# One head of each pair in whole float32 in the first attention stage, and fewer transfers for the score operands

## The chip, the cores and the metric

The kernel runs on one core of one Trainium2 chip. The metric is the device time of one execution in microseconds (us), as the median of several runs. The engines of the core work side by side and meet through semaphores: PE multiplies matrices into PSUM, DVE and ACT read PSUM and SBUF, POOL works on SBUF alone, and SP here issues nearly all transfers, in the fixed order of its queue.

## The reference

Attention for 4 batches of 12 heads, 448 positions and head size 64, followed by two mixers over the joined heads. Only the attention part and the outline of the mixers matter here:

```python
def rmsnorm(x, g):
    rms = np.sqrt(np.mean(x * x, axis=-1, keepdims=True) + 1e-06)
    return x / rms * g
q_n, k_n = (rmsnorm(q, g_q), rmsnorm(k, g_k))
scores = (1.0 / np.sqrt(q.shape[-1])) * np.matmul(q_n, k_n.transpose(0, 1, 3, 2))
attn = np.exp(scores - np.max(scores, axis=-1, keepdims=True))
attn = attn / (np.sum(attn, axis=-1, keepdims=True) + 1e-09)
x = np.matmul(attn, v)          # then (4, 448, 768)
# first mixer:  u = x + (U, V mixing over positions); x = u + relu(u @ w_ch1) @ w_ch2   (768 -> 3072 -> 768)
# second mixer: u = x + relu mixing over positions;   x = u + relu(u @ w_ch1) @ w_ch2   (768 -> 1536 -> 768)
```

The channel weights of the mixers arrive as float64 and are turned into float32 on the chip by a chain on ACT, DVE and POOL (`to_f32`, lines 113 to 135).

## The kernel before, in words

A product that must be good to float32 is made of float32r products. An operand x is split into `hi`, the value rounded to float32r, and `lo`, the rest; a product of two split operands is `hi*hi + lo*hi + hi*lo`, three matmuls that add up in one PSUM bank (lines 523 to 525 for the mixers). A float32r product of 448 columns is one row `128x448` of PE in the profile.

The attention works on pairs of heads: `load_pair` (line 241) loads q, k and v of two heads, normalises q and k (squares and scaling on POOL, sums on DVE), and splits v into `vs` (line 281, ACT and POOL). `turn_pair` (line 284) transposes q and k on PE, splits them out of PSUM (ACT writes `hi`, DVE writes `lo`), and then stacks them by SBUF-to-SBUF transfers on SP: for each head `qs` is [q_hi; q_lo], `ks` is [k_hi; k_hi] and `kt` is [k_lo; k_lo], each 128 partitions of which the upper and the lower 64 are one transfer (lines 310 to 313). That is 12 transfers of 112 KB a pair, and two matmuls of depth 128 then make the scores: `qs*ks + qs*kt` (lines 324 and 325).

`softmax` (line 318) makes, for each of 4 chunks of 112 rows, the scores, the negated maximum on DVE (line 327), the exponential with its sum on ACT (line 329), and scales by the reciprocal on POOL (line 336). `weigh` (line 339) transposes the probabilities on PE into `pt`, 4 blocks of 112x112 a chunk, copies them out as `ph` (ACT, line 363) and `pl = pt - ph` (DVE, line 367), and multiplies twice: `vs` holds v_hi and v_lo side by side in its 128 columns, so `ph*[v_hi, v_lo]` and `pl*[v_hi, v_lo]` give all four parts, and line 375 (ACT) and line 376 (DVE) add the lower half of the result to the upper one.

`weigh` already has a branch for heads named in `whole`: p and v stay in float32 and one matmul a chunk takes the place of two. In the kernel before no pair names any head (lines 750 and 751).

The program has four stages. In the first, the **lone stage**, the 24 heads of batches 0 and 1 run with nothing else beside them but the loads of some weights (until about 213 us). At the seam the first weights of the mixer are loaded and converted and its first products start. In the second stage the mixer of batches 0 and 1 runs on PE, with the 24 heads of batches 2 and 3 spread between its products; then come the second mixer and both mixers of batches 2 and 3.

The order on each engine isn't that of the source: a scheduler of the build simulates the program with its own costs and writes out a fixed order for each engine, SP included. An instruction that must wait holds up all that stand behind it on its engine. Buffers set when that happens: q and k have 2 each, v 3, `vs` 2, the stacked operands 3 each, and the turned `hi` and `lo` one each. The load of v of a later pair (line 247) waits in SP's queue until a buffer of v is free.

Of the kernel before, what the change touches and what calls it, by code (L numbers as in the profile page):

```python
# [10 lines left out]
F32R = mybir.dt.float32r  # L11
U32 = mybir.dt.uint32
I64 = mybir.dt.int64
AF = mybir.ActivationFunctionType
# [10 lines left out]
def attention_then_two_mixers(  # L25
# [30 lines left out]
    nc = tc.nc  # L56
    P = 128
    B, H, S, D = q.shape
    DM = out.shape[2]
    CP, NC4 = 112, 4  # L60
# [14 lines left out]
    def f(x):  # L75
        return x.bitcast(F32)

    def mm(o, l, r, start, stop):
        nc.tensor.matmul(o, lhsT=l, rhs=r, start=start, stop=stop)  # L79
# [20 lines left out]
    pools = {"late": False, "split_u": nc.gpsimd}  # L100
# [140 lines left out]
    def load_pair(b, hp, whole, mul):  # L241
        h0 = 2 * hp
        raw = []
        for nm, src in (("q", q), ("k", k), ("v", v)):
            t = pools["at"].tile([CP, 2, NC4, D], F32, tag=f"{nm}r", bufs=AT[nm + "r"],
                        name=f"{nm}r")
            nc.sync.dma_start(t, src[b, h0:h0 + 2].rearrange("h (p c) d -> p h c d", c=NC4))
            raw.append(t)
        qr, kr, vr = raw

        ms = pools["at"].tile([CP, 2, 8], F32, tag="ms", name="ms")
        for i, t in enumerate((qr, kr)):
            sq = pools["at"].tile([CP, 2 * NC4, D], F32, tag="sq", bufs=AT["sq"], name="sq")
            tt = t.rearrange("p h c d -> p (h c) d")
            mul(sq, tt, tt)
            nc.vector.reduce_sum(ms[:, i], sq, axis=AX.X)
        nc.gpsimd.tensor_scalar(ms, ms, 1.0 / D, 1e-6, op0=ALU.mult, op1=ALU.add)
        rs = pools["at"].tile([CP, 2, 8], F32, tag="rs", name="rs")
        nc.scalar.activation(rs, ms, AF.Ln)
        nc.scalar.activation(rs, rs, AF.Exp, scale=-0.5)  # L260
        nt = pools["at"].tile([CP, 2, 8], F32, tag="nt", name="nt")
        nc.gpsimd.tensor_mul(nt, rs, rs)
        nc.gpsimd.tensor_mul(nt, nt, ms)
        nc.gpsimd.tensor_scalar(nt, nt, -0.5, 1.5, op0=ALU.mult, op1=ALU.add)
        nc.gpsimd.tensor_mul(rs, rs, nt)

        def scale(i, shape):
            return rs[:, i].rearrange("p (h c) -> p h c", h=2).unsqueeze(3).to_broadcast(shape)

        qn, kn = [], []  # L270
        for i, (nm, t, n) in enumerate((("qn", qr, qn), ("kn", kr, kn))):
            n.append(pools["at"].tile([CP, NC4, 2, D], F32, tag=nm, bufs=AT["qn"], name=nm))
            mul(
                n[0].rearrange("p c h d -> p h c d"), t, scale(i, [CP, 2, NC4, D]))
        qn, kn = qn[0], kn[0]

        vs = pools["at"].tile([CP, 2, NC4, 2, D], F32R, tag="vs", bufs=AT["vs"], name="vs")
        js = [j for j in range(2) if j not in whole]
        if js:
            js = slice(js[0], js[-1] + 1)  # L280
            split(vr[:, js], vs[:, js, :, 0], vs[:, js, :, 1])
        return qn, kn, [vr[:, j] if j in whole else vs[:, j] for j in range(2)]

    def turn_pair(qn, kn):

        parts = []
        for n, scale in ((qn, gg), (kn, None)):
            tt = psum("t", [P, S], "tt")
            for c in range(NC4):
                nc.tensor.transpose(  # L290
                    tt[:, c * CP:(c + 1) * CP], n[:, c].rearrange("p h d -> p (h d)"),
                    ident[:CP, :CP])
            hi = pools["at"].tile([P, S], F32R, tag="qh" if scale else "kh",
                                  bufs=1, name="hi")
            lo = pools["at"].tile([P, S], F32R, tag="ql" if scale else "kl",
                                  bufs=1, name="lo")
            if scale:
                nc.scalar.activation(hi, tt, AF.Copy, scale=scale)
                nc.vector.scalar_tensor_tensor(
                    lo, tt, scale, f(hi), op0=ALU.mult, op1=ALU.subtract)  # L300
            else:
                nc.scalar.activation(hi, tt, AF.Copy)
                nc.vector.tensor_sub(lo, tt, f(hi))
            parts += [hi, lo]
        qh, ql, kh, kl = parts
        res = []
        for j in range(2):
            rows = slice(j * D, (j + 1) * D)
            st = []
            for nm, top, low in (("qs", qh, ql), ("ks", kh, kh), ("kt", kl, kl)):  # L310
                t = pools["at"].tile([P, S], F32R, tag=nm, bufs=3, name=nm)
                nc.sync.dma_start(f(t[:D]), f(top[rows]))
                nc.sync.dma_start(f(t[D:]), f(low[rows]))
                st.append(t)
            res.append(st)
        return res

    def softmax(pr, qs, ks, kt):
# [20 lines left out]
    def weigh(pr, vj, j, dst, whole):  # L339

        pv = psum("v", [P, S], "pv")

        def product(kc, ph, pl):
            if whole:
                mm(pv[:D], vj[:, kc], ph, kc == 0, kc == NC4 - 1)
                return
            vk = vj[:, kc].rearrange("p t d -> p (t d)")
            mm(pv, vk, ph, kc == 0, False)
            mm(pv, vk, pl, False, kc == NC4 - 1)

        last = None
        for kc in range(NC4):
            pt = psum("p", [CP, S], "pt")
            for c in range(NC4):
                nc.tensor.transpose(  # L355
                    pt[:, c * CP:(c + 1) * CP], pr[c][:, kc * CP:(kc + 1) * CP],
                    ident[:CP, :CP],
                )
            if last:
                product(*last)  # L360
            ph = pools["pp"].tile([CP, S], F32 if whole else F32R, tag="ph", bufs=AT["ph"],
                                  name="ph")
            nc.scalar.activation(ph, pt, AF.Copy)  # L363
            pl = None
            if not whole:
                pl = pools["pp"].tile([CP, S], F32R, tag="pl", bufs=AT["pl"], name="pl")
                nc.vector.tensor_sub(pl, pt, f(ph))  # L367
            last = kc, ph, pl
            yield
        product(*last)  # L370
        if whole:
            nc.vector.tensor_copy(dst[j * D:(j + 1) * D], pv[:D])
            return
        tmp = pools["at"].tile([D, S], F32, tag="tmp", bufs=1, name="tmp")
        nc.scalar.activation(tmp, pv[D:], AF.Copy)
        nc.vector.tensor_add(dst[j * D:(j + 1) * D], pv[:D], tmp)

    def attention(pairs, seam):

        n = 2 * len(pairs)
        loaded, turned, probs = {}, {}, {}
        dst = None

        def soft(h):
            if not 0 <= h < n:
                return iter(())
            probs[h] = []
            return softmax(probs[h], *turned[h // 2][h % 2])  # L390

        for t in range(-5, n):
            if t == seam:
                for _ in soft(t):
                    pass
            steps = [soft(t + 1) if t + 1 != seam else iter(())]
            if t >= 0:
                if t % 2 == 0:
                    dst = pairs[t // 2][3]()
                steps.append(weigh(  # L400
                    probs.pop(t), loaded[t // 2][2][t % 2], t % 2, dst, t % 2 in pairs[t // 2][2]))
            for _ in zip_longest(*steps):
                pass
            if t >= 0 and t % 2:
                pairs[t // 2][4](dst)
            h = t + 3
            if 0 < h < n and h % 2 == 0:
                turned[h // 2] = turn_pair(*loaded[h // 2][:2])
            h = t + 5
            if h < n and h % 2 == 0:  # L410
                loaded[h // 2] = load_pair(
                    *pairs[h // 2][:3], nc.gpsimd.tensor_mul if h else nc.vector.tensor_mul)
                if h == 0:
                    turned[0] = turn_pair(*loaded[0][:2])
            yield t


# [321 lines left out]
    with ExitStack() as stack:  # L739
# [6 lines left out]
        def new_xo():  # L746
            return pools["at"].tile([P, S], F32, tag="xo", bufs=1, name="xo")

        att = attention(
            [(b, hp, (), lambda xT=xT, hp=hp: xT[:, hp], lambda dst: None)  # L750
             for b, xT in zip((b0, b1), xs) for hp in range(NP)]
            + [(b, hp, (), new_xo,
                lambda dst, b=b, hp=hp: nc.sync.dma_start(xd[b][hp], dst))
# [60 lines left out]
    for _ in ffn("b", wb1, wb2, xs, us, lambda i: None, mid=mid, last=last,  # L814
                 half=lambda i, h: store((b0, b1)[i], xs[i], h)):
# [6 lines left out]
             half=lambda i, h: store((b2, b3)[i], xs[i], h))  # L822
# [31 lines left out]
```

## Time and profile before

| what | value |
|---|---|
| time before, median of 3 runs | 1570.84 us (1570.04 to 1572.85) |
| span of the profiled execution, first to last instruction | 1565.9 us |
| median less that span | 4.9 us |
| mean granted TensorE clock | 0.979 |
| lone stage, first scores to the last sum of a head | 20.84 to 212.91 us |
| PE busy in the whole span | 94% |
| transfers: bytes, mean rate | 180.97 MB, 116 GB/s |

The profile shows one execution. Its span is what the profiler saw between the first and the last instruction; the profiled execution's own time around the span isn't listed, so the median of the timed runs stands beside it. A row of busy time names line, engine and operation, then what is written and read, the shape, how often, and the mean duration of one. Durations on PE are of a pipeline and longer than the distance from one matmul to the next; where the distance matters it is read from the start times of neighbours. "Idle before" is the time in which the engine had nothing to do just before such an instruction, with what ended it.

### The profile page before, as it was taken

To read this page: it belongs to the slowest core of one execution; us is meant where nothing else is said; L and a number is where in the kernel's file an instruction comes from. 1 tells how busy PE (TensorE), PEld (TensorE's weight loads), DVE (VectorE), ACT (ScalarE), POOL (GpSimd) and SP (SyncE) were. 2 spreads that over 40 slices of the span, in tenths; PEclk is the share of its full clock that TensorE was granted. 3 is DMA by queue.
4 is the path that set the end of the run, shared out by engine and by line. 5 is a ranking of instruction groups with operands and counts; after the bars stand their busy time and mean duration, and the time that the engine had idled before them with its cause. 6 is when DMAs were issued, how large, how long until landed. Compare 5 with 4: busy or idle time off the path is not lost.

```text
span 1565.9 us, 21838 instructions
## 1 busy us (share of the span) xinstructions
PE 1467.3 (94%) x7522; PEld 1297.9 (83%) x7522; DVE 1124.4 (72%) x1824; ACT 731.0 (47%) x1449; POOL 824.9 (53%) x844
## 2 busy tenths in 40 slices
PE   5888877999999999999999999899999999999998
PEld 3566756888888889888888998789998999988997
DVE  6787977878888887766958776586756764576653
ACT  5786855666666665443624443342322222342311
POOL 6788886987877655554735543042443523103320
PEclk9898969999999999999999999999999999999999
DMA  6456663565654444542515540511212111101202
GB/s 168 118 143 151 153 198 99 168 190 180 196 161 147 142 146 137 183 172 69 184 39 187 187 143 23 163 58 51 71 51 69 43 51 61 66 21 51 71 21 91
DMA packets 103950, 180.97 MB, mean 116 GB/s; under 512 B 10464, under 2 KB 79552, under 8 KB 103840
## 3 DMA queue, kind: packets, MB, share of 16 engines
q1 hardware_dynamic: 103520, 179.58, 37.2%
q8 instruction: 60, 0.98, 0.3%
q14 instruction: 50, 0.41, 0.1%
q10 hardware_dynamic: 320, 0.00, 0.0%
HBM read 107.19 MB, written 36.57 MB: 92 GB/s over the span
## 4 chain that ended last, share of the span: by engine, by line
PE 65%; DVE 15%; DMA 6%; POOL 5%; ACT 4%; issue 4%; SPq 1%; DVEq 0%; POOLq 0%; ACTq 0%
PE ps_x L79 26%; PE ps_g L79 16%; PE ps_p L79 11%; PE sc L79 3%; PE pv L79 2%; PE pt L355 2%; DVE w_bits L126 2%; PE ps_u L79 2%; DVE w_bits L131 2%; PE ps_t L79 2%; DMA qr<-in_q_dram 1%; POOL w_bits L134 1%; DVE w_bits L127 1%; DVE nm L327 1%; POOL w L145 1%
## 5 line engine op out<-in xcount | busy, mean ns | idle before, releaser
L79 PE MATMUL ps_x<-gs,w 128*128 128x448 f32 x2592 | 576.4, 369 | 14.1 <-DVE xT L656 4.2
L79 PEld LDWEIGHTS ps_x<-gs,w 128*128 128x128 f32 x2592 | 484.0, 189 | 62.0 <-DVE xT L526 8.4
L79 PE MATMUL ps_g<-u,w 128*128 128x448 f32 x1584 | 343.7, 369 | 2.0 <-DVE gs L513 1.5
L79 PEld LDWEIGHTS ps_g<-u,w 128*128 128x128 f32 x1584 | 295.3, 188 | 27.8 <-DVE gs L513 1.9
L145 POOL TENSOR_TENSOR w<-w 128x768 fp32r<-128x768 f32 x44 | 85.0, 1941 | 220.0 <-ACT w L144 153.3
L134 POOL TENSOR_TENSOR w_bits<-w_bits,w_round 128x768 uint32<-128x768 uint32 (+3 forms) x80 | 142.1, 1776 | 93.8 <-DVE w_bits L131 34.0
L145 POOL TENSOR_TENSOR w<-w_bits,w 128x768 fp32r<-128x768 f32 (+3 forms) x82 | 147.8, 1809 | 79.8 <-ACT w L144 76.7
L656 DVE TENSOR_TENSOR xT<-ps_x,xT 128x448 f32<-128x448 f32 x216 | 127.9, 617 | 65.4 <-PE ps_x L79 63.6
L526 DVE TENSOR_TENSOR xT<-ps_x,xT 128x448 f32<-128x448 f32 x216 | 131.9, 616 | 39.5 <-PE ps_x L79 36.8
L336 POOL TENSOR_SCALAR p<-p,sm 112x448 f32<-112x448 f32 x192 | 135.4, 718 | 24.7 <-DVE sm L333 20.9
L329 ACT ACTIVATE p<-sc,nm 112x448 f32<-112x448 f32 x192 | 121.7, 635 | 43.6 <-DVE nm L327 37.3
L145 POOL TENSOR_TENSOR w_a<-w_a 128x384 fp32r<-128x384 f32 (+1 forms) x28 | 41.7, 1490 | 186.0 <-DVE w_t L223 142.9
L367 DVE TENSOR_TENSOR pl<-pt,ph 112x448 fp32r<-112x448 f32 x192 | 116.6, 614 | 16.9 <-ACT ph L363 16.4
L327 DVE TENSOR_REDUCE nm<-sc 112x1 f32<-112x448 f32 x192 | 116.1, 613 | 14.7 <-PE sc L79 14.2
L355 PE MATMUL pt<-ident,p 112*112 112x112 f32 x768 | 116.8, 263 | 3.8 <-POOL p L336 3.4
L363 ACT ACTIVATE ph<-pt 112x448 fp32r<-112x448 f32 x192 | 101.4, 544 | 39.9 <-PE pt L355 38.8
L126 DVE TENSOR_SCALAR w_bits<-w_bits 128x768 f32<-128x768 f32 (+3 forms) x80 | 81.9, 1023 | 47.8 <-ACT w_bits L125 47.4
L355 PEld LDWEIGHTS pt<-ident,p 112*112 112x112 f32 x768 | 92.0, 136 | 24.7 <-POOL p L336 6.7
L627 DVE TENSOR_TENSOR pu<-ps_p,pu 128x448 f32<-128x448 f32 x98 | 59.2, 619 | 70.8 <-PE ps_p L79 70.7
L130 ACT ACTIVATE w_round<-w_raw 128x768 uint32<-128x768 uint32 (+3 forms) x80 | 69.8, 872 | 73.9 <-POOL w_bits L134 71.9
L79 PE MATMUL sc<-ks,qs 128*112 128x448 f32 x192 | 81.5, 436 | 21.5 <-ACT p L329 13.3
L144 ACT ACTIVATE w<-w_bits 128x768 fp32r<-128x768 f32 (+3 forms) x82 | 65.6, 818 | 54.5 <-POOL w_bits L134 32.3
(104 smaller groups left out, 2390.6 us busy)
## 6 DMA issues: line engine op xcount, KB each, us to landing
w_raw<-in_moe_w_ch_dram SPq DMA_DIRECT2D x72, 768.0 KB, 4.4
c_a<-w_bits SPq DMA_DIRECT2D x48, 384.0 KB, 3.1
ks<-hi SPq DMA_DIRECT2D x96, 112.0 KB, 2.3
kt<-lo SPq DMA_DIRECT2D x96, 112.0 KB, 2.3
w<-c_a SPq DMA_DIRECT2D x28, 384.0 KB, 3.7
c_b<-w_bits SPq DMA_DIRECT2D x24, 384.0 KB, 3.1
w_a<-c_a SPq DMA_DIRECT2D x20, 384.0 KB, 2.9
w<-c_b SPq DMA_DIRECT2D x16, 384.0 KB, 3.5
```

The source lines that it names most:

```text
L79: nc.tensor.matmul(o, lhsT=l, rhs=r, start=start, stop=stop)
L126: nc.vector.tensor_scalar_max(f(w), f(w), TINY)
L134: nc.gpsimd.tensor_tensor(w, w, r, op=ALU.add)
L145: nc.gpsimd.tensor_sub(lo, w, f(hi))
L327: nc.vector.tensor_reduce(nm, sc, axis=AX.X, op=ALU.max, negate=True)
L329: nc.scalar.activation(p, sc, AF.Exp, bias=nm, accum_out=sm[:, c % 2:c % 2 + 1])
L336: nc.gpsimd.tensor_scalar(x, x, sm[:, i:i + 1], 1.0, op0=ALU.mult, op1=ALU.mult)
L355: nc.tensor.transpose(pt[:, c * CP:(c + 1) * CP], pr[c][:, kc * CP:(kc + 1) * CP], ident[:CP, :CP],)
L363: nc.scalar.activation(ph, pt, AF.Copy)
L367: nc.vector.tensor_sub(pl, pt, f(ph))
L526: nc.vector.tensor_add(xT[:, dc], px, xT[:, dc])
L656: nc.vector.tensor_add(xT[:, dc], px, xT[:, dc])
```

## The change

In the lone stage head 0 of each pair is `whole`: v of that head isn't split, p isn't split, and one float32 matmul a chunk (48 in all) takes the place of two float32r ones. Its weights are 128 columns wide (the chunk and the 64 columns behind it), of which only the first 64 rows of the result are used. The copy `ph` out of PSUM goes to ACT for even chunks and to DVE for odd ones. In all pairs of both stages the turned operands lie in one tile `both` (hi and lo side by side), and `ks` holds [k_hi | k_lo] in both halves: two transfers of 224 KB a head where there were four of 112 KB, so 8 a pair. The first pair still moves k in 8 transfers of 112 KB (12 a pair).

```diff
+        flat = vr.rearrange("p h c d -> p (h c d)")
+        return qn, kn, [flat[:, j * NC4 * D:] if j in whole else vs[:, j] for j in range(2)]
...
-            hi = pools["at"].tile([P, S], F32R, tag="qh" if scale else "kh",
-                                  bufs=1, name="hi")
-            lo = pools["at"].tile([P, S], F32R, tag="ql" if scale else "kl",
-                                  bufs=1, name="lo")
+            both = pools["at"].tile([P, 2, S], F32R, tag="qq" if scale else "kk",
+                                    bufs=1, name="both")
+            hi, lo = both[:, 0], both[:, 1]
...
-            for nm, top, low in (("qs", qh, ql), ("ks", kh, kh), ("kt", kl, kl)):
-                t = pools["at"].tile([P, S], F32R, tag=nm, bufs=3, name=nm)
-                nc.sync.dma_start(f(t[:D]), f(top[rows]))
-                nc.sync.dma_start(f(t[D:]), f(low[rows]))
+            qs = pools["at"].tile([P, S], F32R, tag="qs", bufs=3, name="qs")
+            ks = pools["at"].tile([P, 2, S], F32R, tag="ks", bufs=3, name="ks")
+            for u in range(2):
+                half = slice(u * D, (u + 1) * D)
+                if not first:
+                    nc.sync.dma_start(f(ks[half]), f(kk[rows]))
+                nc.sync.dma_start(f(qs[half]), f(qq[rows, u]))
+            if first:
+                for i in range(2):
+                    for u in range(2):
+                        nc.sync.dma_start(f(ks[u * D:(u + 1) * D, i]), f(kk[rows, i]))
+            res.append((qs, ks[:, 0], ks[:, 1]))
...
-                mm(pv[:D], vj[:, kc], ph, kc == 0, kc == NC4 - 1)
+                mm(pv, vj[:, kc * D:kc * D + P], ph, kc == 0, kc == NC4 - 1)
...
+            if whole and kc % 2:
+                nc.vector.tensor_copy(ph, pt)
+            else:
+                nc.scalar.activation(ph, pt, AF.Copy)
...
-            [(b, hp, (), lambda xT=xT, hp=hp: xT[:, hp], lambda dst: None)
+            [(b, hp, (0,), lambda xT=xT, hp=hp: xT[:, hp], lambda dst: None)
```

On PE, the products of the first head (`pv`) in the order before, where `vs` is the split v; between them stand transposes of p (`pt`) and scores (`sc`):

```order
L79 MATMUL pv<-ph,vs 128x448
L355 MATMUL pt<-ident,p 112x112 x4
L79 MATMUL sc<-ks,qs 112x448
L79 MATMUL sc<-kt,qs 112x448
L79 MATMUL pv<-pl,vs 128x448
L79 MATMUL pv<-ph,vs 128x448
```

And now, where `vr` is v as it was loaded:

```order
L79 MATMUL pv<-ph,vr 128x448
L360 MATMUL pt<-ident,p 112x112 x4
L79 MATMUL pv<-ph,vr 128x448
L360 MATMUL pt<-ident,p 112x112 x6
L79 MATMUL sc<-ks,qs 112x448 x6
L360 MATMUL pt<-ident,p 112x112
L79 MATMUL pv<-ph,vr 128x448
```

Each chunk of a whole head has one product, and none that waits for DVE's `pl`.

On SP, the stretch from one load of v to the next in the lone stage, before (`qs`, `ks`, `kt` are the stacked operands, `hi` and `lo` the turned ones):

```order
L247 DMA vr<-in_v_dram 112x2x256 x2
L247 DMA qr<-in_q_dram 112x2x256
L247 DMA kr<-in_k_dram 112x2x256
L312 DMA qs<-hi 64x448 x2
L313 DMA qs<-lo 64x448 x2
L312 DMA ks<-hi 64x448
L313 DMA ks<-hi 64x448
L312 DMA kt<-lo 64x448
L313 DMA kt<-lo 64x448
```

(The four `ks` and `kt` of the second head follow in the same way, and then the next `vr`.) And now:

```order
L247 DMA vr<-in_v_dram 112x2x256
L247 DMA qr<-in_q_dram 112x2x256
L247 DMA kr<-in_k_dram 112x2x256
L315 DMA qs<-both 64x448 x4
L314 DMA ks<-both 64x896 x4
```

The four transfers of `ks` carry what eight carried, and the load of v still stands ahead of the loads of q and k and of the stacking.

## Rows read from the trace of the kernel before

**Rows 1.** Busy time by stretch (us and instructions), granted clock, DMA share, GB/s
```profile
20.84:212.91 192.07, 159.33 (x874) 120.44 (x874) 157.94 (x325) 149.06 (x385) 159.33 (x279) 0.93 0.61 151
250.00:575.00 325.00, 311.52 (x1702) 276.93 (x1703) 273.79 (x462) 210.29 (x436) 245.66 (x265) 0.99 0.55 168
```

**Rows 2.** The same view, two pieces of the lone stage
```profile
60.00:80.00 20.00, 14.38 (x63) 9.89 (x62) 13.32 (x27) 12.18 (x33) 14.26 (x28) 0.74 0.77 180
160.00:180.00 20.00, 17.87 (x109) 13.92 (x107) 19.93 (x44) 18.52 (x53) 16.83 (x32) 1.00 0.65 160
```

**Rows 3.** Chain that ended last, 20 to 213 us, by line
```profile
by line: issue 11.0%; PE sc L79 10.9%; DMA qr<-in_q_dram 7.0%; DVE nm L327 6.7%; DVE pl L367 6.6%; PE pv L79 5.9%; PE pt L355 5.4%; DMA ks<-hi 4.7%; POOL p L336 4.6%; ACT p L329 4.2%; ACT ph L363 3.1%; POOL sq L255 2.8%; DMA w_raw<-in_moe_w
```

**Rows 4.** Groups by line, 20 to 213 us: busy, mean ns, idle before
```profile
L355 PE MATMUL pt<-ident,p 112*112 112x112 f32 x384 | 58.7, 268 | 3.0 <-POOL p L336 2.7 <-POOL rs L265 0.3
L367 DVE TENSOR_TENSOR pl<-pt,ph 112x448 fp32r<-112x448 f32 x96 | 57.9, 614 | 6.3 <-ACT ph L363 6.2
...
L363 ACT ACTIVATE ph<-pt 112x448 fp32r<-112x448 f32 x96 | 50.3, 546 | 17.4 <-PE pt L355 16.8
...
L79 PE MATMUL sc<-ks,qs 128*112 128x448 f32 x96 | 42.0, 460 | 15.0 <-DMA ks<-hi 7.6 <-ACT p L329 6.9 <-DVE pl L367 0.3
L79 PE MATMUL pv<-pl,vs 112*128 112x448 f32 x96 | 41.7, 434 | 4.7 <-DVE pl L367 4.5
...
L79 PE MATMUL sc<-kt,qs 128*112 128x448 f32 x96 | 36.7, 413 | 1.2 <-DMA kt<-lo 1.2
...
L145 POOL TENSOR_TENSOR vs<-vr,vs 112x512 fp32r<-112x512 f32 x12 | 15.4, 1282 | 0.2
L376 DVE TENSOR_TENSOR xT<-pv,tmp 64x448 f32<-64x448 f32 x24 | 14.7, 611 | 7.7 <-ACT tmp L375 7.5
...
L375 ACT ACTIVATE tmp<-pv 64x448 f32<-64x448 f32 x24 | 13.0, 541 | 0.8 <-PE pv L79 0.3
```

**Rows 5.** Groups by line, 20 to 195 us, a DVE operation within SBUF
```profile
L126 DVE TENSOR_SCALAR w_bits<-w_bits 128x448 f32<-128x448 f32 x1 | 0.4, 380 | 0.0
```

**Rows 6.** Timeline of PE at full clock: start, us, instruction
```profile
101.38 0.36 PE L79 MATMUL pv<-pl,vs 112*128 112x448 f32 x1
101.58 0.55 PE L355 MATMUL pt<-ident,p 112*112 112x112 f32 x4
101.89 0.45 PE L79 MATMUL pv<-ph,vs 112*128 112x448 f32 x1
```

**Rows 7.** Timeline of SP's queue, one pair of the lone stage: issues
```profile
101.48 0.31 SPq L247 DMA_DIRECT2D kr<-in_k_dram  x1
102.29 1.11 SPq L312 DMA_DIRECT2D qs<-hi  x2
...
107.53 0.59 SPq L312 DMA_DIRECT2D ks<-hi  x1
108.17 0.60 SPq L313 DMA_DIRECT2D ks<-hi  x1
...
109.47 0.60 SPq L313 DMA_DIRECT2D kt<-lo  x1
```

**Rows 8.** Transfers, 20 to 213 us: KB each, median us to landing
```profile
ks<-hi SPq DMA_DIRECT2D x52, 112.0 KB, 2.3
qr<-in_q_dram SPq DMA_DIRECT2D x14, 224.0 KB, 3.0
```

**Rows 9.** Waits of SP's queue, 20 to 213 us: total, times, longest
```profile
SPq L247 <- POOL qn L273: 16.7, 7, 4.3
SPq L247 <- POOL vs L145: 15.5, 5, 11.8
```

**Rows 10.** The chain at the seam: start, us, what
```profile
197.28 5.49 DMA qr<-in_q_dram
...
210.12 5.42 DMA w_raw<-in_moe_w_ch_dram
...
226.86 1.01 PE ps_h L79 x2
```

More of the change, by code (lines that the diff above doesn't have):

```diff
@@ L281, in load_pair, with turn_pair @@
             split(vr[:, js], vs[:, js, :, 0], vs[:, js, :, 1])
-        return qn, kn, [vr[:, j] if j in whole else vs[:, j] for j in range(2)]
-    def turn_pair(qn, kn):
+        flat = vr.rearrange("p h c d -> p (h c d)")
+        return qn, kn, [flat[:, j * NC4 * D:] if j in whole else vs[:, j] for j in range(2)]
+    def turn_pair(qn, kn, first=False):
         parts = []
@@ L303, in turn_pair @@
                 nc.vector.tensor_sub(lo, tt, f(hi))
-            parts += [hi, lo]
-        qh, ql, kh, kl = parts
+            parts.append(both)
+        qq, kk = parts
         res = []
@@ L308, in turn_pair @@
             rows = slice(j * D, (j + 1) * D)
-            st = []
-            for nm, top, low in (("qs", qh, ql), ("ks", kh, kh), ("kt", kl, kl)):
-                t = pools["at"].tile([P, S], F32R, tag=nm, bufs=3, name=nm)
-                nc.sync.dma_start(f(t[:D]), f(top[rows]))
-                nc.sync.dma_start(f(t[D:]), f(low[rows]))
-                st.append(t)
-            res.append(st)
+            qs = pools["at"].tile([P, S], F32R, tag="qs", bufs=3, name="qs")
[10 more added lines that the diff above has]
+            res.append((qs, ks[:, 0], ks[:, 1]))
         return res
@@ L362, in weigh @@
                                   name="ph")
-            nc.scalar.activation(ph, pt, AF.Copy)
+            if whole and kc % 2:
+                nc.vector.tensor_copy(ph, pt)
+            else:
+                nc.scalar.activation(ph, pt, AF.Copy)
             pl = None
@@ L413, in attention @@
                 if h == 0:
-                    turned[0] = turn_pair(*loaded[0][:2])
+                    turned[0] = turn_pair(*loaded[0][:2], first=True)
             yield t
```

## The prediction

> **What bounds the kernel now.** I read the busy time by stretch first. In the lone stage, 192.07 us long, no engine is full: POOL is busy for 159.33, DVE for 157.94, ACT for 149.06, and PE for 159.33 by a record that counts overlapping matmuls [rows 1]. The reader should see four engines within 7% of each other and some 33 us in which even the busiest one waits. In the second stage PE is busy for 311.52 of 325.00 us [rows 1], so there only PE's own work sets the pace.
>
> PE's record has to be corrected. At full clock two products of 448 columns start 0.20 us apart, and four transposes of p take 0.31 us of PE's order [rows 6]. The lone stage has 384 such products (96 each of sc with ks, sc with kt, pv with ph and pv with pl) and 384 transposes of p [rows 4]: 384 x 0.20 + 96 x 0.31 = 107 us, and the transposes of q and k, 13 pairs of 8, add 8 at the same pitch. So PE needs about 115 of 192 us. It has room; DVE, POOL and ACT have little.
>
> Second, two pieces of that stage: between 160 and 180 us DVE is busy for 19.93 of 20 us at a granted clock of 1.00; between 60 and 80 us DVE has 13.32, PE's clock falls to a mean of 0.74 (a mix of its levels 1.2 and 2.4 GHz) and the transfers are busy for 0.77 [rows 2]. So there are stretches paced by DVE and stretches paced by transfers. Third, the chain says the same: DVE's two lines nm and pl hold 13.3%, pv on PE 5.9%, transfers of q 7.0% and of ks 4.7% [rows 3].
>
> **The change part by part.** The sum is made against the profiled span, 1565.9 us; the median of the timed runs lies 4.9 us above it, and I add the same to the result.
>
> *The vector engines.* 12 whole heads with 4 chunks lose 48 `pl` of 0.614 us on DVE and 24 `ph` of 0.546 us on ACT, and DVE gains 24 copies [rows 4]. No row shows such a copy. The nearest from above is `pl`, 0.614, which reads the same PSUM bank; from below an operation within SBUF of that size, 0.380 [rows 5]. I take 0.614, since PSUM is what is read. DVE: -48 x 0.614 + 24 x 0.614 = -14.7 us (down to -20.4 at 0.380). The copy in place of the last sum has that sum's shape and counts as equal. ACT: -24 x 0.546 - 12 x 0.541 (`tmp`) = -19.6. POOL: 12 splits of v at 1.28 us become half as large, -7.7 [rows 4]; if a fixed part stays, less.
> What of this is on the path? The stage ends when the least relieved of the full engines ends. If POOL alone paced it, the stage would gain 7.7 and the 33 us of waiting would stay; if DVE did, 14.7. They are equally busy and the chain has more of DVE, so I take the middle, -11, and keep 0 and -20.4 as ends.
>
> *The whole product.* 48 whole products take the place of 96 at 0.20 us, 19.2 us. The trace has no such product. From below, it could cost one float32r product, 0.20. From the rows on the other side, the mixers make one product that is good to float32 with three float32r ones, 0.60. I take 0.60, since the arithmetic has the same job: 48 x 0.60 = 28.8, so PE gains 9.6 us. PE has 77 us of room, so most is hidden beside DVE and POOL; what is exposed I take from the chain, where pv holds 5.9% of 193 us, 11.4 us, of the 38.4 us that its 192 products take: 0.30. So +2.8 us; ends: -2.8 (at 0.20, 9.6 less) and +9.6 (all exposed). A wait also goes: no product of such a head stands behind `pl` any more (4.5 us of PE's idle time for both heads [rows 4]); what is late next is `ph` itself, so I count nothing.
> The Trainium skill (FP8 and Floating Point Precision, section TensorE Precision Notes) says that a true float32 product goes through the array four times, high and low parts against each other. No run shows it yet; worked out from that page, one product would be about 0.80 us, an estimate, and the term would be 0.30 x 48 x (0.80 - 0.40) = +5.8 instead of +2.8, which turns the sum below into -8.2.
>
> *The stacking.* SP takes 0.64 us from one issue to the next, and a pair's 12 issues run from 102.29 to 110.07 us, 7.8 us [rows 7]; one of them lands in 2.3 us [rows 8]. Eight issues take 5.1 if a transfer of twice the bytes is issued as fast. The nearest row for that, a load of 224 KB, takes 0.31 on SP [rows 7], so bytes don't set it; if they did, 7.8 would stay. PE's idle time until ks and kt land is 7.6 + 1.2 = 8.8 us [rows 4]; a third shorter burst gives -3, ends 0 and -8.8. Against that, ks now leaves when `lo` is done too, one DVE operation (0.6 us) after `hi`; but kt had to wait for it before, and each chunk's scores need both. The tile `both` comes free for the next pair when all 4 ks transfers have landed, as before.
> In the Trainium skill (DMA: Bandwidth & Descriptors, section Issuing engines are not separate DMA queues) the time a sequencer spends on issuing is called usually small beside the transfer; by that, fewer issues would be worth nothing and the sum would be 3 less. This trace disagrees: 7.8 us of issuing stand against 2.3 us to land [rows 7, 8].
>
> *The second stage.* 12 pairs lose four transfers each. PE is busy for 96% there [rows 1], so I count nothing; the 13 us it is idle bound a gain. Its order is written anew, which I can't price.
>
> *The sum.* -11 + 2.8 - 3 = -11.2: a span of 1554.7, and 1559.6 us as timed, say 1560.
>
> **The rivals.**
> *The load of v holds SP's queue (slower).* v of a whole head is read by PE's products to the last, so its buffer comes free at the end of a head, not after a split. The next v stands on SP ahead of the loads of q and k and the stacking of a pair. Now SP waits for the split of v 5 times, 15.5 us, 3.1 each, the longest 11.8 [rows 9]. If all 11 loads behind the first waited 3.1, that would be 34 us, 18.6 more, and where it reaches the chain through q (already 7.0% of it [rows 3]) the end is -11.2 + 18.6: 1578 us. It decides from 1.0 us more per pair. For it: transfers of q are on the chain as it is. Against: there are 3 buffers, and a buffer's next use is three pairs on.
>
> *The seam swallows it (no change).* The first mixer product waits for a chain that starts with a load of q (5.49 us at 197.28) and goes on through a weight's load (5.42 us at 210.12) to the first product of the rank mix at 226.86 [rows 10]. None of that gets shorter. If the weights' chain rather than the heads sets when the second stage starts, at most 3 us are left, 1568 to 1573, say 1570. Against: the scheduler keeps these loads in program order behind the loads of pairs, so they should move forward with them.
>
> *The stalls close as well (faster by more).* If DVE is what counts throughout (-14.7), all of PE's waits for ks and kt go (-8.8), and the clock, at a mean of 0.74 between 60 and 80 us [rows 2], stays up so that the whole products cost nothing at the end, the time is 1547.
>
> **How the numbers follow.** The forecast 0.56, its own range 1551 to 1568; v holding SP 0.16; the seam 0.13; more than the sum 0.15. A change below 0.2%, 3.1 us, can't be told from none in this kernel. Faster: 0.55 of the forecast and the 0.15, 0.70. Same: 0.12 of the seam case and 0.01 of the forecast, 0.13. Slower: 0.16 and 0.01 of the seam case, 0.17. The range 1546 to 1576 takes in nearly all of the forecast, the seam, and the nearer halves of the other two.
>
> **What would show it.** Right: the lone stage some 11 us shorter to the last sum of a head; DVE's and ACT's busy time there down by about 15 and 20 us with POOL the fullest; one whole product 0.6 us (0.8 by the page) in the start times on PE; a pair's burst on SP near 5 us; the second stage as long as before. Wrong: the loads of q on SP late behind a wait for pv would be the first rival; a lone stage that is shorter with the first mixer products at the same time, the second; a burst still at 7.8 us or a whole product over 1 us would break the terms of the sum.

## The result, and the profile after

The changed kernel takes 1556.14 us (median of 4 runs, 1552.11 to 1559.57) against 1570.44 for the kernel before (1566.81 to 1572.85): 14.3 us less, a ratio of 0.991 with a 95% interval of 0.989 to 0.993. The forecast was 1560. The profiled execution of the changed kernel is the slowest of its four (1559.57 us, a span of 1556.9), so the two traces differ by 9.0 us where the medians differ by 14.3. Where the time went is read from the traces, by marks: the last sum of a head in the lone stage, the first product of the mixer (where its row on PE starts), the last sum of a head in the second stage, the end.

| kernel | lone stage ends | first mixer product | second stage ends | span |
|---|---|---|---|---|
| before | 212.9 | 230.0 | 623.3 | 1565.9 |
| changed | 197.0 | 211.3 | 613.5 | 1556.9 |

So the lone stage ends 15.9 us sooner, and the first mixer product comes 18.7 us sooner (18.5 by the row of its weight load). The second stage, from that product to its last sum, is 402.2 us where it was 393.3: 8.9 us are given back. From there to the end 0.8 us is added.

The busy times by stretch of the changed kernel (us and count on PE, PE's weight loads, DVE, ACT, POOL; granted clock, DMA share, GB/s), the lone stage and the second one, answer to [rows 1]:

```profile
19.70:197.00 177.30, 157.64 (x874) 114.36 (x874) 144.50 (x297) 127.69 (x348) 149.72 (x282) 0.98 0.65 160
211.30:613.50 402.20, 383.32 (x2068) 339.99 (x2068) 327.46 (x551) 251.58 (x516) 286.85 (x302) 0.98 0.52 158
```

In the lone stage DVE fell by 13.4 us, ACT by 21.4 and POOL by 9.6; PE's record hardly moved while the stage became 14.8 us shorter, so PE now has the largest share by this record, and the mean granted clock rose from 0.93 to 0.98. The record counts overlapping matmuls; counted as the prediction counts it, PE needs 115 - 96 x 0.20 + 48 x 0.75 = 132 of the 177 us, less than POOL's 149.72. (Four transposes of p were taken there as 0.31 us. By their own row, 0.55 us for four where one has 0.27 [rows 4, 6], they start 0.09 apart and take 0.38; that makes it some 123 us before and 140 now, still less than POOL's.) The chain by line shows the same change of hands, against [rows 3]:

```profile
by line: PE pv L79 19.3%; PE sc L79 14.0%; PE pt L360 10.7%; DMA ks<-both 8.9%; issue 6.1%; DMA qs<-both 5.4%; DVE nm L332 3.6%; SPq L314 3.2%; PE tt L291 3.0%; ACT p L334 3.0%; ACT ph L371 2.7%; DVE pl L375 2.6%; POOL p L341 1.9%; DMA kr<-
```

pv went from 5.9% to 19.3%, nm and pl from 13.3% to 6.2%. Next the groups by line of the same stretch (busy, mean ns, idle before), against [rows 4]:

```profile
L79 PE MATMUL sc<-ks,qs 128*112 128x448 f32 x192 | 60.2, 418 | 11.0 <-ACT p L334 5.6 <-DMA ks<-both 4.2 <-issue 0.8
...
L79 PE MATMUL pv<-ph,vr 112*128 112x448 f32 x96 | 45.8, 559 | 3.2 <-DVE ph L369 2.9 <-ACT ph L371 0.3
...
L375 DVE TENSOR_TENSOR pl<-pt,ph 112x448 fp32r<-112x448 f32 x48 | 29.0, 613 | 2.5 <-ACT ph L371 2.5
...
L369 DVE COPY ph<-pt 112x448 f32<-112x448 f32 x24 | 14.8, 617 | 4.6 <-PE pt L360 4.5
...
L145 POOL TENSOR_TENSOR vs<-vr,vs 112x256 fp32r<-112x256 f32 x10 | 7.3, 731 | 0.9 <-ACT vs L144 0.6
```

The copy on DVE takes 0.617 us, as assumed. Half the split of v takes 0.731 where the whole took 1.282, so a split saves 0.55, not 0.64. PE's wait for the stacked keys fell from 8.8 to 4.2 us. Each whole product leaves two records, 96 for 48. How long one holds PE is read from start times on PE (start, us, what), at full clock:

```profile
105.51 0.92 PE L79 MATMUL pv<-ph,vr 112*128 112x448 f32 x2
106.26 0.55 PE L360 MATMUL pt<-ident,p 112*112 112x112 f32 x4
```

From one start to the next instruction it is 0.75 us, where two float32r products took 0.40 [rows 6]. SP's queue around the stacking of a pair (start, us of issuing, what), against [rows 7]:

```profile
62.15 2.39 SPq L315 DMA_DIRECT2D qs<-both  x4
66.64 0.32 SPq L247 DMA_DIRECT2D vr<-in_v_dram  x1
67.82 2.75 SPq L314 DMA_DIRECT2D ks<-both  x4
```

The eight issues take 2.39 + 2.75 = 5.14 us, four of 112 KB and four of 224 KB; with the load of v and the waits between them they end 8.4 us after the first began. The transfers themselves land later (KB, median us), against [rows 8]:

```profile
ks<-both SPq DMA_DIRECT2D x50, 224.0 KB, 4.0
qs<-both SPq DMA_DIRECT2D x50, 112.0 KB, 2.3
```

### The profile page after: what moved, and what is told of

It is laid out like the page before. It is cut to its first block, busy times and chain, and to the rows that moved or that the text cites. A ratio compares the mean times of both kernels' runs of the same rounds, so it can differ in the third digit from the quotient of the medians.

```text
span 1556.9 us, 21606 instructions
## 1 busy us (share of the span) xinstructions
PE 1465.8 (94%) x7522; PEld 1295.5 (83%) x7522; DVE 1101.6 (71%) x1800; ACT 708.8 (46%) x1413; POOL 813.9 (52%) x844
## 4 chain that ended last, share of the span: by engine, by line
PE 65%; DVE 11%; DMA 7%; POOL 6%; ACT 5%; issue 4%; SPq 1%; ACTq 0%; POOLq 0%; DVEq 0%
PE ps_x L79 26%; PE ps_g L79 14%; PE ps_p L79 10%; PE pv L79 3%; PE sc L79 3%; PE pt L360 2%; POOL w_bits L134 2%; PE ps_u L79 2%; DMA c_a<-w_bits 2%; PE ps_t L79 2%; DVE w_bits L126 2%; POOL w L145 1%; DMA ks<-both 1%; DVE w_bits L131 1%; DMA qs<-both 1%
## 5 line engine op out<-in xcount | busy, mean ns | idle before, releaser
L79 PE MATMUL ps_x<-gs,w 128*128 128x448 f32 x2592 | 577.7, 371 | 14.7 <-DVE xT L664 4.2
L79 PE MATMUL sc<-ks,qs 128*112 128x448 f32 x384 | 118.7, 402 | 18.8 <-ACT p L334 13.4
L360 PE MATMUL pt<-ident,p 112*112 112x112 f32 x768 | 111.5, 260 | 4.5 <-POOL p L341 3.4
L126 DVE TENSOR_SCALAR w_bits<-w_bits 128x768 f32<-128x768 f32 (+3 forms) x80 | 75.5, 943 | 45.5 <-ACT w_bits L125 45.3
L371 ACT ACTIVATE ph<-pt 112x448 fp32r<-112x448 f32 (+1 forms) x168 | 88.2, 544 | 35.8 <-PE pt L360 35.1
L375 DVE TENSOR_TENSOR pl<-pt,ph 112x448 fp32r<-112x448 f32 x144 | 87.3, 615 | 11.1 <-ACT ph L371 10.8
L125 ACT ACTIVATE w_bits<-w_raw 128x768 f32<-128x768 f32 (+3 forms) x80 | 69.9, 876 | 53.3 <-POOL w L145 36.5
```

What stands on the lines that cost most here:

```text
L126: nc.vector.tensor_scalar_max(f(w), f(w), TINY)
L360: nc.tensor.transpose(pt[:, c * CP:(c + 1) * CP], pr[c][:, kc * CP:(kc + 1) * CP], ident[:CP, :CP],)
```

## The experiments

Each was timed beside the kernel before in the same session. The changed kernel itself was timed in the first session alone; where a run is compared with it in us, two sessions are compared, in which the kernel before had medians of 1567.23 to 1571.32 us. Because the build writes a new order for all engines at any edit, the time of one edit is read twice: as the ratio, and by the marks of its trace.

**Whole heads alone.** The changed kernel with `turn_pair` as before:

```diff
-    def turn_pair(qn, kn, first=False):      # 8 transfers a pair
+    def turn_pair(qn, kn):                   # 12 transfers a pair, lines 284 to 316 of the kernel before
```

> One head of each pair is whole as in the changed kernel, but the score operands are stacked by 12 transfers a pair as before. Theory A (both parts pay, as in my sum: engines' relief -11, PE +2.8 to +5.8, stacking -3): 5 to 8 us faster than before, 1562 to 1565, and the lone stage 8 to 11 us shorter than 192. Theory B (the stacking carries the gain, since the trace after has a whole product at 0.75 us and PE's 17 us more eat the relief): within 3 us of before, 1568 to 1573. Theory C (the whole heads carry all of it): 1555 to 1559.

1577.35 us against 1570.64, a ratio of 1.005 (1.003 to 1.007): slower, which none of the three theories had. Its lone stage ends at 210.7, 2.2 us sooner than before; the first mixer product comes at 226.0, and the second stage takes 404.0 us. DVE and ACT are relieved in the lone stage (145.92 and 130.83 us busy) and the time is hardly shorter; the longer products on PE are part of this run too. One stretch of SP's queue shows how loads and stacking come late:

```profile
101.30 9.31 SPq L247 DMA_DIRECT2D vr<-in_v_dram  x2
...
113.95 0.47 SPq L313 DMA_DIRECT2D qs<-hi  x1
...
129.36 0.60 SPq L314 DMA_DIRECT2D kt<-lo  x1
```

The first row's 9.31 us are two loads of v, issued in 0.31 us each, and between them a wait of 8.6 us for PE's products `pv`. Behind it the 24 score transfers of two pairs go out back to back from 113.95 to 129.96 us: one pair takes 8 us of SP however late it is. PE's busy time and the granted clock in the same stretch:

```profile
110.00:120.00 10.00, 5.90 (x32) 4.04 (x31) 6.20 (x10) 4.66 (x11) 8.71 (x16) 0.86 0.57 159
120.00:130.00 10.00, 9.17 (x35) 6.38 (x35) 7.58 (x16) 7.16 (x21) 7.44 (x16) 0.63 0.72 165
```

PE is busy for 5.90 of the first 10 us, and over the next 10 its clock has fallen to a mean of 0.63, a mix of its two levels.

**Stacking alone.** The kernel before with the new `turn_pair`:

```diff
-    parts += [hi, lo]                        # 12 transfers a pair
+    parts.append(both)                       # 8 transfers a pair, 12 for the first; no whole heads
```

> Only the stacking by 8 transfers a pair (12 for the first), no whole head. Theory A: 3 us faster, 1566 to 1569, with a burst on SP of 5 us where it was 7.8. Theory B (the stacking carries the gain): 1555 to 1560. Theory C (the whole heads carry all): 1569 to 1572.

1570.0 us, ratio 1.000 (0.997 to 1.002). The lone stage ends at 210.6, 2.3 us sooner, with DVE busy for 160.17 and POOL for 159.53 us of its 189.5. PE's wait for the stacked keys there is 8.0 us where it was 8.8. So in the lone stage one part alone gives 2.2, the other 2.3, and both together 15.9. A sum of parts can't describe that.

**All copies on ACT.** The changed kernel with

```diff
-            if whole and kc % 2:
+            if False:
```

> The changed kernel with all copies ph of the whole heads on ACT: DVE loses 24 copies of 0.6 us (14.7 us), ACT gains 24 of 0.55 (13.1 us). Theory A (DVE and POOL set the pace, ACT has room, 128 of 177 us busy in the lone stage): 0 to 7 us faster than the changed kernel, 1549 to 1556. Rival (ACT's order, with exp behind the copies, is the path): 3 to 8 us slower than the changed kernel, 1559 to 1564.

1566.63 us, ratio 0.998 (0.996 to 1.000), some 10 us slower than the changed kernel. Both theories look for the difference in the wrong place: the lone stage ends at 197.2, as in the changed kernel, although DVE has 11 us less and ACT 10 more to do there. The second stage, whose work isn't touched by this edit, takes 410.3 us in place of 402.2.

**Whole products twice.**

```diff
-                mm(pv, vj[:, kc * D:kc * D + P], ph, kc == 0, kc == NC4 - 1)
+                for i in range(2):
+                    mm(pv, vj[:, kc * D:kc * D + P], ph, kc == 0 and i == 0, kc == NC4 - 1 and i == 1)
```

> The changed kernel with each whole product issued twice into the same sum, so the result of these heads is doubled: PE gains 48 x 0.75 = 36 us in the lone stage, nothing else changes. Theory A (PE is exposed by 0.30 of what it gains): 11 us slower than the changed kernel, 1567. Rival (PE is the bound of the lone stage after the change): 30 to 36 us slower, 1586 to 1592. Rival (PE's work is hidden): under 4 us slower, 1556 to 1560.

1585.53 us, ratio 1.011 (1.008 to 1.013), 29 us over the changed kernel. The lone stage ends at 220.8, 23.8 us later for 48 x 0.75 = 36 us more on PE: 0.66 of it is exposed, not 0.30, and not all, with the reserve that the two builds' orders differ. The stretch, for comparison with the changed kernel's above:

```profile
20.00:220.80 200.80, 190.19 (x970) 134.16 (x970) 147.99 (x302) 131.73 (x351) 155.32 (x290) 0.99 0.59 144
```

**Whole heads alone, four buffers of v.**

```diff
-    AT = dict(qr=2, kr=2, vr=3, qn=1, vs=2, p=8, ph=3, pl=3, sq=1)
+    AT = dict(qr=2, kr=2, vr=4, qn=1, vs=2, p=8, ph=3, pl=3, sq=1)     # on the first experiment
```

> Whole heads without the new stacking, as the first experiment, which was 0.5% slower than before, and with four buffers of v in place of three, so that a load of v need not wait for PE's last product of a whole head. Theory A (v held SP's queue there: its waits for pv and pt were 33 us in the lone stage, and behind them stood q and the stacking): 8 us or more faster than the first experiment, 1562 to 1569, the lone stage under 185 us and the granted clock there above 0.95. Rival (the 12 transfers themselves, or PE's own work, hold it): within 3 us of the first experiment, 1574 to 1580.

1567.62 us, ratio 0.997 (0.995 to 0.999). By its time theory A would hold (10 us faster than the first experiment); by its trace it falls. The lone stage ends at 209.0 and is 188.3 us long at a clock of 0.94, not under 185 at above 0.95, and SP waits for pv longer than in the first experiment (40.0 us against 23.5). The first mixer product even comes at 231.5. The gain is behind it: from the first mixer product to the last sum of the first two mixers, 747 us, against 764 in the first experiment, with the same work in both.

**The changed kernel, four buffers of v.** The same edit on the changed kernel.

> The changed kernel with four buffers of v. In its trace SP waits 14.4 us for pv before loads of v. Theory A (v's hold still costs there): 3 to 8 us faster than the changed kernel, 1548 to 1553. Rival (with 8 transfers a pair SP has the room to make it up): within 2 us of the changed kernel, 1554 to 1558.

1561.18 us, ratio 0.994 (0.992 to 0.995). The lone stage ends at 199.0; SP's wait for pv falls from 14.4 to 10.8 us. No gain; but three quarters of that wait are left, so this says little of what the rest of it costs.

**Two weight chunks earlier.** The changed kernel with

```diff
+            if t == 2 * H - 5:
+                pools["late"] = True
+                w1s = [w1_chunk("a", wa1, j) for j in range(G)]
+                pools["late"] = False
             if t == 2 * H - 1:
                 break
```

and without these lines behind the loop.

> The changed kernel with the first two weight chunks of the first mixer loaded four heads earlier, inside the lone stage. Between 211 and 400 us the changed kernel loses some 10 of the 18.5 us by which its first mixer product came sooner. Theory A (the supply of converted weights holds the start of the second stage): the mixer's products lead from the start, 4 to 10 us faster than the changed kernel, 1546 to 1552. Rival (what is taken early costs the lone stage as much on POOL and DVE): 1555 to 1560.

1569.16 us, ratio 0.999 (0.998 to 1.001), some 13 us slower than the changed kernel. The lone stage ends at 208.3, 11.3 us later, and the mixer doesn't lead: 468 of its products have begun by 400 us, 499 in the changed kernel, 462 before. The conversions cost the lone stage what they could save: over it POOL is busy for 163.1 us and DVE for 152.8, 13.4 and 8.3 more than in the changed kernel.

**Whole heads in the second stage too.**

```diff
-            + [(b, hp, (), new_xo,
+            + [(b, hp, (0,), new_xo,
```

> The changed kernel with head 0 of each pair whole in the second stage too. PE sets the pace there, so 48 whole products of 0.75 us in place of 96 of 0.20 should cost all of the difference. Theory A (what is a gain beside DVE and POOL is a loss where PE is the bound): 48 x 0.35 = 17 us slower than the changed kernel, 1573. Rival (the waits for pl, and DVE's part in the conversion of weights, pay for it): under 6 us slower, 1556 to 1562.

1572.26 us, ratio 1.001 (0.999 to 1.003), 16 us slower than the changed kernel, as theory A had it: by 620 us the mixer has begun 1123 products where the changed kernel has 1189, and 66 x 0.20 = 13 us.

**Whole heads alone, v of three pairs.** The first experiment, in which pairs 3 to 11 use v of the first three again:

```diff
+            if nm == "v" and b < 2 and len(kept_v) == 3:
+                raw.append(kept_v[hp % 3])
+                continue
...
+            if nm == "v" and b < 2:
+                kept_v.append(t)
```

> Whole heads with 12 transfers a pair, and in the lone stage v is loaded for the first three pairs alone; the later nine pairs multiply by these three again (their results are of the wrong v), so no load of v stands in SP's queue behind PE. Judged by the last sum of a head in the lone stage (212.9 us before, 210.7 with whole heads alone, 197.0 in the changed kernel). Theory A (loads of v behind PE's products hold SP, and with it q and the stacking): it ends at 195 to 200, at a granted clock of 0.96 or more. Theory B (SP's 12 issues a pair hold it): 205 to 211, the clock at 0.93 to 0.95.

1571.13 us, ratio 1.003 (1.001 to 1.005). The lone stage ends at 210.5 at a clock of 0.94: theory A falls by its range. It isn't a clean test: with the loads of v gone SP waits at the other loads instead, 51.2 us for POOL's `qn` in three waits.

**The kernel before, v of three pairs.** The same edit on the kernel before.

> The kernel before with v loaded for three pairs alone in the lone stage, as in the experiment beside it (nine pairs use the wrong v): what the loads of v cost there without whole heads. Theory A (they cost only behind PE's products): the lone stage ends at 210 to 213 as before. Rival (they cost in any case, 11 loads of 224 KB at 60% busy transfers): 200 to 207, and then the experiment beside it says little.

1578.23 us, ratio 1.007 (1.004 to 1.010), its lone stage ends at 223.7. Fewer transfers and a later end: the order that was written anew is the likely cause, in which SP waits 48.2 us for POOL's `qn` where it waited 16.2 (20 to 200 us), but this isn't shown. So these two can't price the loads of v; they only show that without them the lone stage isn't short.

**Whole heads alone, 12 transfers from two queues.** The first experiment, with

```diff
+                q_ = nc.scalar if j and nm != "qs" else nc.sync
-                nc.sync.dma_start(f(t[:D]), f(top[rows]))
-                nc.sync.dma_start(f(t[D:]), f(low[rows]))
+                q_.dma_start(f(t[:D]), f(top[rows]))
+                q_.dma_start(f(t[D:]), f(low[rows]))
```

> Whole heads with 12 transfers a pair of the old size, of which four (ks and kt of the second head) are issued from ACT, so SP issues 8 a pair as in the changed kernel, and ACT gains some 2 us of issuing a pair in place of what it lost. Judged by the lone stage. Theory B (the number of issues in SP's one queue is what the stacking mends): it ends at 196 to 201. Theory A (the loads of v behind PE hold SP) or the size of the packets (1.8 KB against 3.6 KB a row): 205 to 211.

1557.6 us against 1567.23, ratio 0.994 (0.993 to 0.996), and the lone stage ends at 198.8, 11.9 us sooner than with the same 12 transfers from SP alone. The stretches of this kernel, and below of whole heads with all 12 on SP:

```profile
21.50:198.80 177.30, 160.95 (x874) 115.24 (x874) 143.17 (x296) 126.67 (x346) 150.09 (x280) 0.97 0.62 157
```
```profile
20.30:210.70 190.40, 169.42 (x874) 121.23 (x874) 145.92 (x298) 130.83 (x348) 150.67 (x282) 0.93 0.59 147
```

DVE, ACT and POOL are busy for the same time in both within 4.2 us; the transfers have the same size and number. The edit changes the queue alone, and with it the order that the build writes; the stage is 13.1 us shorter at a clock of 0.97 in place of 0.93, and PE's record of the same products is 8.5 us shorter. New orders alone haven't moved the lone stage that far in kernels with whole heads: three builds with all 12 transfers on SP need 188.3 to 190.6 us for it (two of them with other buffers or loads of v), six with 8 on SP and the same work there, this one among them, 177.0 to 179.8 us. Theory B is borne out: with the bytes, the packets and the loads of v as they were, taking four issues a pair off SP's single row gives nearly what the stacking gives. Whether it's their number or the second queue's own order isn't separated.

**The first pair by 8.**

```diff
-                    turned[0] = turn_pair(*loaded[0][:2], first=True)
+                    turned[0] = turn_pair(*loaded[0][:2])
```

> The changed kernel with 8 transfers for the first pair too, in place of 12. The first scores then need a transfer of 224 KB that leaves only when lo is done. Theory A (it costs at the start alone): first scores 0.3 to 1 us later than 19.7, the time within 2 us of the changed kernel, 1554 to 1559. Rival (the order on the engines is dealt anew, which by the other runs moves the second stage by several us): 5 us or more to either side, while the lone stage stays within 2 us of 197.

1562.55 us, ratio 0.998 (0.996 to 0.999): 6 us slower than the changed kernel by the medians, some 10 by the ratios. The first scores begin at 24.3 us in place of 19.7 and the lone stage ends at 204.1, 7.1 later. Both theories missed: the cost at the start is larger than that of a later transfer. In SP's queue the loads of the next pair now stand between the stacked q and k of the first:

```profile
15.02 2.46 SPq L315 DMA_DIRECT2D qs<-both  x4
17.57 0.54 SPq L247 DMA_DIRECT2D qr<-in_q_dram  x1
...
18.88 2.88 SPq L314 DMA_DIRECT2D ks<-both  x4
```

In the changed kernel k's transfers begin at 16.75.

## Why the prediction was right, and where not

*The range, the sign and the main place.* The lone stage was to be 11 us shorter and ends 15.9 us sooner; the median fell by 14.3 where 11.2 was forecast. That the two lie so near is in part luck: the whole product cost more than its term, the stacking gained more beside the whole heads, and the second stage, counted at nothing, gave some of it back. How much it gives back hangs on the build: three others whose lone stage ends within 2 us of this one take 1557.6 to 1566.63 us.

*The vector engines* were sized well: DVE -13.4 (forecast -14.7), ACT -21.4 (-19.6), POOL -9.6 (-7.7). That the stage gains about the middle of DVE's and POOL's relief isn't confirmed: with that relief, the longer products and 12 transfers on SP it gains 2.2, and no run has the relief without the longer products. In the changed kernel 11 us less of DVE change nothing (197.2 with all copies on ACT).

*The stacking* was priced at -3 beside the rest. Alone it gives 2.3 in the lone stage, so the number holds by itself, but not its reason: PE's wait for the stacked keys was to fall by a third from 8.8 us and fell to 8.0. Beside whole heads the stacking is worth 13.7 us (210.7 to 197.0). What failed is the step "the sum": it adds terms that aren't independent. The two-queue run shows that with whole heads SP's row of issues holds the stage; that before the change the vector engines hold it as well, at about 210, is argued from their busy times and from the little that stacking alone gives. The 2.3 us are less than a new order can do: another build without whole heads, with fewer loads of v, ends at 223.7. How SP holds the stage is partly argued too: its issues, added up, take 110 of the 192 us before and 108 of 190 with whole heads alone, so it is never full; no wait of one kind carries it (waits for pv, for the buffers of q, and the back-to-back burst change places from build to build), and the two queues give a second order as well as fewer issues in a row. One cost was put at nothing and shows: `ks` now leaves when `lo` is done, and SP waits 13.0 us for that (line 303) where it waited 0.8.
The Trainium skill (DMA: Bandwidth & Descriptors, section Issuing engines are not separate DMA queues) says that initiating DMAs on several engines saves only the sequencer's time for it, usually small beside the DMA itself. For one transfer the trace agrees: some 0.6 us of issuing against 2.3 us to land. The prediction set twelve issues, 7.8 us, against the landing of one, which isn't the same comparison. What the runs add is the row: with four of a pair's twelve issues on another queue the stage ends 11.9 us sooner.

*The whole product* was mis-sized: 0.60 was taken, 0.75 measured, and the exposed share was taken from the chain before, 0.30, where doubling the products in the changed kernel shows 0.66. With both, the term is 48 x 0.35 x 0.66 = +11 in place of +2.8, and the sum would be -3. The chain before was a bad measure for a path that the change itself makes: pv's share of it goes from 5.9% to 19.3%.
The Trainium skill (FP8 and Floating Point Precision, section TensorE Precision Notes) says that true float32 takes four passes through the array. The trace comes near it: 0.75 us is 3.75 times the 0.20 us from one float32r product to the next, and the estimate made from that page was 0.80.

*The second stage* was counted at nothing and took back 8.9 us in the profiled pair. By the last sum of the first two mixers, 979.0 us before and 972.6 now, 12.3 of the 18.7 us are gone, and 2.6 are won behind it. The rival of the seam named the right place for some of it, though its sign, a first mixer product at the same time, didn't come: by 250 us the changed kernel's mixer has begun 48 products, the one before 36, a lead of 2.4 us in products of 0.20 us where 18.7 us in time had been won; by 400 us it is 499 against 462, 7.4 us. In the changed kernel's chain from 255 to 300 us the saving of converted weights appears twice:

```profile
257.55 2.85 PE ps_g L79 x14
...
276.52 7.95 DMA c_a<-w_bits
286.54 4.75 PE ps_g L79 x17
...
299.26 5.72 DMA c_a<-w_bits
```

That fits a mixer that waits for its weights, but loading them earlier didn't win it back, and other builds whose second stage does the same work take 393.9 us (stacking alone) to 410.3 (copies on ACT). What part is the supply of weights and what part the order that the build happens to write stays open.

*The rival of v holding SP* shows its sign, 14.4 us of waits for pv at SP's loads where the kernel before has none, but not its price: the time fell, and with the loads of v as they were the two-queue run still wins 11.9 us. A fourth buffer doesn't help the changed kernel, and without the loads the lone stage with 12 transfers is as long, though neither run takes SP's waits away.

## What to carry to other kernels

Where several engines are busy for about the same share, don't add the gains of two edits: ask what each would run into alone, and try both together before giving up one that gives nothing by itself. Count the issues in the queue as an engine of its own, and look at their order as well as their sum: with whole heads, 12 issues a pair from one queue kept this stage at 188 us and more, 8 let it end in 180 or less, though the queue was issuing for little more than half of the time. And where a scheduler rewrites the whole order at each edit, compare builds by marks in the trace, since a stage that the edit doesn't touch can move by 16 us.

## What the runs showed of the hardware

A float32 product of 448 columns holds PE for 0.75 us and appears as two records. A transfer of 224 KB within SBUF is issued nearly as fast as one of 112 KB (four in 2.75 against four in 2.39 us) but lands in 4.0 us against 2.3. The mean granted clock of the lone stage was 0.93 before, 0.93 to 0.94 with whole heads and 12 transfers on SP, 0.97 with the stacking alone or with two queues, and 0.98 in the changed kernel. It doesn't tell the stage's length by itself: with the stacking alone it is 0.97, and the stage ends at 210.6.
